# A wider moving side for two small products at the ends of a decode kernel: 448 columns at once, folded back by float32 selecting matmuls

## The chip, the core and the metric

One core of one Trainium2 chip runs the whole program in one launch. The metric is the time of one execution on the device in microseconds (us). A core has TensorE (PE in the profile, its weight loads as PEld), VectorE (DVE), ScalarE (ACT), GpSimd (POOL) and SyncE (SP), which run side by side and wait for one another through semaphores, and 16 DMA engines that bring data from HBM to the on-chip memory SBUF. Matmul results go to PSUM banks.

## What is computed

One decode step for two sequences (B = 2), all in bfloat16 outside the accumulations. A layer norm of x feeds two branches: attention over the last 2,048 positions of a K and a V cache with 16 query heads on 8 key heads of width 256, and a small feed-forward net (FFN). The FFN's output gates that of the attention:

```python
xn = _layernorm(x)                                   # x: 2 x 1 x 448
q  = (xn @ wq)                                       # 16 heads of 256
s  = softmax(q k^T * 256**-0.5) v   @ wo             # last 2048 of 8192 keys; wo: 4096 x 448
g  = silu(relu(xn @ w1) @ w2)                        # w1: 448 x 1792, w2: 1792 x 448
out = x + s * g
```

The caches' part that is read is 8 blocks of 4 MB, and the weights are wq 3.5 MB, w1 and w2 1.5 MB each, and wo 3.5 MB: 44 MB in all, of which every byte is used once.

## The kernel before

The program is a list of operations for each engine, written out by hand: `pr.op` and `pr.dma` append to an engine's list with the operations they depend on, and each engine works through its own list in order. Nothing is planned or reordered by a program.

**The stream of loads.** All large loads go through SP's queue in this order: wq, w1, w2, K block 0, K block 1, V0, K2, V1, K3, V2, V3, and wo in four parts of rows (`WO_PARTS`, a row being 448 numbers on each of 128 partitions). There are two K buffers and two V buffers; V0's buffer holds w1 and w2 first, V1's holds wq. So the issue of V0 waits for the FFN (`st["F"]`), K2 for the last transpose of block 0, V2 for the last product of block 0, and so on. wo is written to K2's buffer and waits for the last transpose of block 2.

**Head.** After the layer norm, `do_q` makes the queries, `do_H` the FFN's hidden layer, `do_hT` turns it, `do_F` (the FFN product with w2) multiplies, and `do_gate` makes silu of it. `do_F` has four column tiles: the array's output columns are split in four groups of 32 partitions, and tile i takes the i-th quarter (112) of the 448 columns. A row of w2 is four matmuls of 112 moving columns, and the result lies with quarter i of sequence b on partition 32i + 16b. The gate is then four operations on 128 x 112. They stand in the middle of block 0: `do_gate()` follows the fifth transpose.

**Four blocks of attention.** For block k, `do_T` transposes K in eight pieces on VectorE, `do_S` makes the scores behind each piece (32 matmuls of 512 columns), `chain` does the softmax (row maximum, its spread by two small matmuls, exponential, transpose), and `do_PV` multiplies with V in 32 matmuls of 512 columns on four column tiles. In `chain(k, pv)` the products with V of the block before stand on TensorE between the softmax's steps. `do_osb`, `do_oT` and `do_at` scale a block's output, fold its heads and spread it into `at_exp`; `do_at` is four VectorE operations of 128 x 16.

**Tail.** After the last V block come `do_PV(3)`, `do_osb`, `do_oT`, `do_at`, two matmuls that gather `at_exp`, a copy `at2`, and the product with wo: 32 rows, each of four matmuls of 112 columns on the four column tiles, accumulated in bank `fbk`. A part of wo is waited for at its first row. Then two VectorE operations (times the gate, plus x) and the store.

```python
for j in range(32):
    deps = deps + [landed.get(j)]
    for i in range(4):
        lo = j * D + i * NCOL
        m_o = pr.op(PE, mm(fbk[32 * i:32 * i + 17, 0:NCOL], view(at2, j, [[2, 17]]),
                           wo_sb[:, lo:lo + NCOL], j == 0, j == 31, tile_position=(0, 32 * i)), deps)
```

Matmuls are recorded by the profile under line 249, that of the helper `mm`, so they are told apart by their tiles.

Of the kernel before, what the change touches and what calls it, by code (L numbers as in the profile page):

```python
# [6 lines left out]
F32 = mybir.dt.float32  # L7
ACT = mybir.ActivationFunctionType
ALU = mybir.AluOpType
AX = mybir.AxisListType  # L10

PE, DVE, ACTE, SP, POOL = "pe", "dve", "act", "sp", "pool"
# [62 lines left out]
def bass_recurrent_scan__sliding_block_cached__dense_activation_relu__decode_kernel(  # L75
# [11 lines left out]
    B, Sq, D = A_x.shape  # L87
# [12 lines left out]
    SLOTS = 7  # L100
    HC = HD // 2
    FC = DFF // 2
    WO_PARTS = [17, 9, 4, 2]
    NCOL = D // 4
    QW = 24 + 8 * 128
    BIG = 1e30
# [2 lines left out]
    with es:  # L109
        pr = _Prog(nc, es)  # L110

        def named(name, shape, dt):
            return es.enter_context(nc.sbuf_tensor(name, shape, dt))

        def psum(name, shape, dt):
            return es.enter_context(nc.psum_tensor(name, shape, dt))

        def view(t, off, dims, n=128, p0=0, pstep=1):
            width = t.shape[1]
            return bass.AP(t, p0 * width + off, [[width * pstep, n]] + dims)  # L120
# [9 lines left out]
        qmask = named("qmask", [128, 4], F32)  # L130
        fold = named("fold", [128, 32], BF)
# [10 lines left out]
        h_n = named("h_n", [128, FC], BF)  # L142
        h_sb = named("h_sb", [128, 32], BF)
        x_c = named("x_c", [128, NCOL], BF)
        ea = named("ea", [128, NCOL], F32)
        g_sb = named("g_sb", [128, NCOL], F32)
        tmp = named("tmp", [128, NCOL], F32)
        out_sb = named("out_sb", [128, NCOL], BF)
# [8 lines left out]
        o_sb = [named(f"o_sb{i}", [128, 512], BF) for i in range(2)]  # L157
        at_exp = named("at_exp", [128, 256], BF)
        at2 = named("at2", [128, 64], BF)
# [3 lines left out]
        wq_sb, w12, wo_sb = vbuf[1], vbuf[0], kbuf[0]  # L163
        W2 = SLOTS * FC
        assert SLOTS * HC <= ROW and W2 + 14 * D <= ROW and 32 * D <= ROW

        sbk = [psum(f"sbk{i}", [128, 512], F32) for i in range(2)]
        obk = [psum(f"obk{i}", [128, 512], F32) for i in range(2)]
        fbk = psum("fbk", [128, 512], F32)
        mbk = psum("mbk", [128, 512], F32)  # L170
        nbk = psum("nbk", [128, 512], F32)
# [18 lines left out]
        def load_v(k):  # L190
            d_v[k] = pr.dma(SP, vbuf[k % 2][:, :], kv_src(k, A_v_cache),
                            [(st["F"], st["q_mm"])[k] if k < 2 else st["PV", k - 2]])
# [7 lines left out]
            out=ident[:, :], in_=ident[:, :], compare_op=ALU.not_equal, fill=1.0,  # L200
# [3 lines left out]
            out=ident_f[:, :], in_=ident_f[:, :], compare_op=ALU.not_equal, fill=1.0,  # L204
            base=0, pattern=[[-1, 128]], channel_multiplier=1), [i1])
        p_one = pr.op(POOL, lambda e: e.memset(one_f[:, :], 1.0), [p_idf])
        p_hz = pr.op(POOL, lambda e: e.memset(h_sb[:, :], 0.0))
# [7 lines left out]
            out=sd[0:B, 0:1], in0=st2[0:B, 1:2], scalar1=EPS, scalar2=None, op0=ALU.add), [v_ag])  # L215
        a_sd = pr.op(ACTE, lambda e: e.activation(sd[0:B, 1:2], sd[0:B, 0:1], ACT.Sqrt), [v_ve])
        v_rs = pr.op(DVE, lambda e: e.reciprocal(rstd[0:B, :], sd[0:B, 1:2]), [a_sd])
        for e2 in range(2):
            v_xn = pr.op(DVE, lambda e, e2=e2: e.tensor_scalar(  # L219
                out=view(xg, 128 - 127 * e2, [[256, 4], [128, 2], [2, 64]], n=B),  # L220
                in0=view(x_sb, 3 * e2, [[1, 4], [0, 2], [SLOTS, 64]], n=B),
# [3 lines left out]
            out=par2[:, :], in_=view(ident, 0, [[1, 2], [2, 64]]), axis=AX.X, op=ALU.add), [p_id])  # L225
# [5 lines left out]
            out=view(wcol, 0, [[4, 128], [1, 4]], n=4), in0=view(ident, 0, [[0, 128], [1, 4]], n=4),  # L231
            scalar1=1.0, scalar2=BIG, op0=ALU.subtract, op1=ALU.mult))
        v_qm = pr.op(DVE, lambda e: e.tensor_reduce(
            out=qmask[:, :], in_=view(ident, 0, [[32, 4], [1, 32]]), axis=AX.X, op=ALU.add))
# [3 lines left out]
                return e.tensor_reduce(out=fold[:, :], in_=view(ident, 0, [[1, 32], [32, 4]]), axis=AX.X, op=ALU.add)  # L238
        v_fold = pr.op(DVE, fold_op)

        def fold8_op(e):
            with nc.allow_low_precision("zeros and ones"):
                return e.tensor_reduce(out=fold8[:, :], in_=view(ident, 0, [[1, 8], [8, 16]]), axis=AX.X, op=ALU.add)
# [4 lines left out]
        def mm(out_ap, lhsT, rhs, start, stop=False, **kw):  # L248
            return lambda e: e.matmul(out_ap, lhsT=lhsT, rhs=rhs, start=start, stop=stop,  # L249
                                      skip_group_check=True, **kw)  # L250

        for s in range(SLOTS):
# [3 lines left out]
            out=view(xr, 0, [[4, SLOTS], [2, 2], [1, 2]]), in0=view(mbk, 0, [[2, SLOTS], [0, 2], [1, 2]]),  # L256
            in1=view(par8, 0, [[1, SLOTS], [1, 2], [0, 2]]), op=ALU.mult), [m_xr, v_par8])

        st = {"mbk": v_xr}
# [28 lines left out]
        def do_qbd(k):  # L288
            deps = [st["qall"], p_qz, st.get(("S", k - 2, 7))]
            for a in range(4):  # L290
                for b in range(2):
                    st["qbd", k] = pr.op(POOL, lambda e, a=a, b=b: e.tensor_copy(  # L292
                        view(qbd[k % 2], 24 + 32 * a + 4 * b, [[2, 2], [128, 8], [1, 2]], n=32, p0=32 * a),
                        view(qall, 32 * k + 16 * b, [[128, 2], [2, 8], [1, 2]], n=32, p0=32 * a)), deps)
                    deps = []
# [12 lines left out]
        def do_hT():  # L308
            deps = [st["h_n"]]
            for j in range(7):  # L310
                o = pr.op(PE, mm(fbk[:, 4 * j:4 * j + 4], view(h_n, j, [[7, 128]], n=4), ident[0:4, 0:4], j == 0), deps)
                deps = []
            st["hT"] = pr.op(DVE, lambda e: e.tensor_copy(
                view(h_sb, 0, [[1, 7], [7, 2], [16, 2]]), view(fbk, 0, [[4, 7], [2, 2], [1, 2]])), [o, p_hz])

        def do_F():
            deps = [d_w2, st["hT"]]
            for f in range(14):
                for i in range(4):
                    lo = W2 + f * D + i * NCOL  # L320
                    o = pr.op(PE, mm(fbk[32 * i:32 * i + 17, 0:NCOL], h_sb[:, f:f + 17],
                                     w12[:, lo:lo + NCOL],
                                     f == 0, f == 13, tile_position=(0, 32 * i)), deps)
                    deps = []
            st["F"] = o

        def do_gate():
            a_e = pr.op(ACTE, lambda e: e.activation(ea[:, :], fbk[:, 0:NCOL], ACT.Exp, scale=-1.0), [st["F"]])
            v_d = pr.op(DVE, lambda e: e.tensor_scalar(
                out=ea[:, :], in0=ea[:, :], scalar1=1.0, scalar2=None, op0=ALU.add), [a_e])  # L330
            v_rc = pr.op(DVE, lambda e: e.reciprocal(tmp[:, :], ea[:, :]), [v_d])  # L331
            st["g"] = pr.op(DVE, lambda e: e.tensor_tensor(
                out=g_sb[:, :], in0=fbk[:, 0:NCOL], in1=tmp[:, :], op=ALU.mult), [v_rc])

        def words(t):
            return t[:, :].bitcast(F32).tensor
# [83 lines left out]
        def do_oT(k):  # L420
            deps = [st["osb", k], v_fold, st["nbk"]]
            for dhi in range(2):
                for t2 in range(2):
                    lo = 256 * t2 + 128 * dhi
                    o = pr.op(PE, mm(nbk[:, 8 * dhi:8 * dhi + 8], o_sb[k % 2][:, lo:lo + 128],
                                     fold[:, 8 * t2:8 * t2 + 8], dhi == 0 and t2 == 0, dhi == 1 and t2 == 1), deps)
                    deps = []
            st["oT", k] = o

        def do_at(k):  # L430
            for b in range(2):
                for h in range(2):
                    st["at", k] = st["nbk"] = pr.op(DVE, lambda e, b=b, h=h: e.tensor_tensor(  # L433
                        out=view(at_exp, 128 * b + 64 * h + 16 * k, [[4, 2], [8, 2], [1, 4]]),
                        in0=view(nbk, 4 * b + 2 * h, [[8, 2], [1, 2], [0, 4]]),
                        in1=view(qmask, 0, [[0, 2], [0, 2], [1, 4]]), op=ALU.mult), [st["oT", k], v_qm])

        def chain(k, pv=None):
            ch_max(k)
# [21 lines left out]
        do_hT()  # L461
        do_F()
        load_v(0)
        do_qbd(0)
        do_qbd(1)
        for e in range(8):
            do_T(0, e)
            do_S(0, e)
            if e == 4:
                do_gate()  # L470
        load_k(2)
        load_v(1)
        for e in range(8):
# [30 lines left out]
        for q in range(8):  # L504
            do_PV(3, q)
        do_osb(3)
        do_oT(3)
        do_at(3)

        d_wo = []  # L510
        j0 = 0
        for n in WO_PARTS:
            d_wo.append((j0, pr.dma(SP, wo_sb[:, j0 * D:(j0 + n) * D], wo_src[:, j0 * D:(j0 + n) * D], [st["T", 2, 7]])))
            j0 += n

        deps = [st["at", NQ - 1], v_fold]
        for b in range(2):
            m_at = pr.op(PE, mm(mbk[:, 256 + 32 * b:288 + 32 * b], at_exp[:, 128 * b:128 * b + 128],
                                fold[:, :], b == 0, b == 1), deps + [st["mbk"]])
            deps = []  # L520
        v_at2 = pr.op(DVE, lambda e: e.tensor_copy(at2[:, :], mbk[:, 256:320]), [m_at])  # L521
        deps = [v_at2, st["g"]]
        landed = dict(d_wo)
        for j in range(32):
            deps = deps + [landed.get(j)]
            for i in range(4):
                lo = j * D + i * NCOL
                m_o = pr.op(PE, mm(fbk[32 * i:32 * i + 17, 0:NCOL], view(at2, j, [[2, 17]]),
                                   wo_sb[:, lo:lo + NCOL],
                                   j == 0, j == 31, tile_position=(0, 32 * i)), deps)  # L530
                deps = []
        v_t = pr.op(DVE, lambda e: e.tensor_tensor(  # L532
            out=tmp[:, :], in0=fbk[:, 0:NCOL], in1=g_sb[:, :], op=ALU.mult), [m_o, st["g"]])
        v_o = pr.op(DVE, lambda e: e.tensor_tensor(  # L534
            out=out_sb[:, :], in0=tmp[:, :], in1=x_c[:, :], op=ALU.add), [v_t, d_xc])
# [33 lines left out]
```

## Time and profile before

| | |
|---|---|
| time, median of 3 runs | 110.56 us (110.33 to 110.9) |
| the profiled execution | 110.73 us |
| its span, first to last instruction | 109.3 us |
| busy in the span | PE 63.9, PEld 26.0, DVE 57.6, ACT 12.4, POOL 9.0 us |
| DMA | 44.19 MB, 404 GB/s over the span |

The span is what the trace covers; 1.43 us of the execution lie around it. A busy time is the union of an engine's instructions, and busy time that runs beside a longer chain costs nothing. In rows of the timeline a bracket tells how long the engine was idle before the row and what released it; "x32" counts instructions that follow one another.

### The profile page before, as it was taken

Reading aid. Unit: us, or ns where it says so; the run is one execution under the profiler, and the core shown is the slowest. Engines: PE = TensorE matmul, PEld = TensorE weight load, DVE = VectorE, ACT = ScalarE, POOL = GpSimd, SP = SyncE. Lnnn points to the kernel's source line nnn. Section 1 sums busy time; section 2 is a strip of 40 time slices with the busy share of each in tenths; the row PEclk is TensorE's granted clock in tenths of the full one; section 3 lists DMA queues with packets and bytes.
Section 4 is the critical chain, followed back from the end, with each engine's and each line's share of the span. In section 5 each row is a group of like instructions: output and inputs, shape, how many; then the busy total and the mean of one; then the engine's idle time right before and its main releaser. Section 6 shows DMA issues by size and latency. Waiting matters only on the chain.

```text
span 109.3 us, 1328 instructions
## 1 busy us (share of the span) xinstructions
PE 63.9 (58%) x554; PEld 26.0 (24%) x554; DVE 57.6 (53%) x95; ACT 12.4 (11%) x24; POOL 9.0 (8%) x45
## 2 busy tenths in 40 slices
PE   0010655764089897849481999683089949009491
PEld 0000113133033222323130334241034214003190
DVE  2165047320399999987435999242399943100202
ACT  2970000000000000200050000032000004100200
POOL 6500000720000004000500000000000000000000
PEclk9999999999556999999996559999959999955559
DMA  6898999999999999999999999999999999999940
GB/s 169 346 483 355 431 404 510 408 432 504 390 396 444 492 396 396 456 480 396 399 480 438 396 408 492 432 396 408 504 420 396 420 498 408 396 405 414 407 171 1
DMA packets 2321, 44.19 MB, mean 404 GB/s; under 512 B 266, under 2 KB 396, under 8 KB 908
## 3 DMA queue, kind: packets, MB, share of 16 engines
q1 hardware_dynamic: 2288, 44.11, 94.6%
q8 instruction: 4, 0.07, 0.2%
q10 hardware_dynamic: 28, 0.01, 0.0%
q14 instruction: 1, 0.01, 0.0%
HBM read 44.11 MB, written 0.00 MB: 403 GB/s over the span
## 4 chain that ended last, share of the span: by engine, by line
DMA 70%; DVE 12%; PE 12%; SPq 3%; issue 1%
DMA kbuf<-in_A_k_cache_dram 42%; DMA kbuf<-in_A_wo_dram 28%; DVE kt L343 10%; PE sbk L249 9%; SPq L36 3%; PE obk L249 2%; DVE tmp L331 1%; DVE rm L361 1%; PE mbk L249 0%; PE nbk L249 0%; PE fbk L249 0%; DVE mx L371 0%; DVE tmp L532 0%; PE mbk L366 0%; DVE out_sb L534 0%
## 5 line engine op out<-in xcount | busy, mean ns | idle before, releaser
L249 PE MATMUL sbk<-kt,qbd 128*128 128x512 bf16 x128 | 36.2, 432 | 15.0 <-DVE kt L343 14.5
L343 DVE STREAM_TRANSPOSE kt<-kbuf 128x1024 f32<-128x1024 f32 x32 | 36.9, 1210 | 8.9 <-DMA kbuf<-in_A_k_cache_dram 8.7
L249 PEld LDWEIGHTS sbk<-kt,qbd 128*128 128x128 bf16 x128 | 12.3, 107 | 37.2 <-DVE kt L343 22.5
L249 PE MATMUL obk<-vbuf,pt 128*16 128x512 bf16 x128 | 9.3, 442 | 4.6 <-DMA vbuf<-in_A_v_cache_dram 4.6
L292 POOL COPY qbd<-qall 32x32 bf16<-32x32 bf16 x32 | 5.7, 204 | 44.1 <-PE sbk L249 28.3
L383 ACT ACTIVATE bias<-mbk 128x1 f32<-128x1 f32 x4 | 0.7, 171 | 58.6 <-PE mbk L249 58.6
L433 DVE TENSOR_TENSOR at_exp<-nbk,qmask 128x16 bf16<-128x16 f32 x16 | 1.7, 166 | 10.5 <-PE nbk L249 10.5
L249 PE MATMUL obk<-vbuf,xr 128*4 128x512 bf16 x28 | 3.2, 626 | 3.8 <-DMA vbuf<-in_A_wq_dram 3.8
L392 DVE STREAM_TRANSPOSE pt<-e_sb 128x512 bf16<-128x512 bf16 x4 | 2.8, 711 | 4.7 <-ACT e_sb L387 4.7
L271 DVE TENSOR_SCALAR kt<-obk 128x1024 bf16<-128x1024 f32 x2 | 2.4, 1218 | 5.6 <-PE obk L249 5.6
L249 PEld LDWEIGHTS obk<-vbuf,pt 128*16 128x16 bf16 x128 | 3.1, 98 | 8.5 <-DMA vbuf<-in_A_v_cache_dram 4.7
L249 PE MATMUL mbk<-ident,xg 2*128 2x2 bf16 x7 | 0.3, 164 | 7.9 <-DVE xg L219 7.9
L361 DVE TENSOR_REDUCE rm<-sbk 128x1 f32<-128x512 f32 x4 | 2.7, 682 | 4.0 <-PE sbk L249 4.0
L249 PE MATMUL fbk<-vbuf,xr 128*4 128x448 bf16 x14 | 4.3, 461 | 0.7 <-DVE h_n L304 0.7
L416 ACT ACTIVATE o_sb<-obk,rs 128x512 bf16<-128x512 f32 x4 | 2.7, 687 | 11.1 <-PE obk L249 11.1
L249 PE MATMUL fbk<-kbuf,at 128*17 128x112 bf16 x128 | 3.1, 282 | 0.4 <-DVE at L521 0.3
L249 PEld LDWEIGHTS fbk<-kbuf,at 128*17 128x17 bf16 x128 | 2.7, 128 | 0.7 <-DVE at L521 0.4
L304 DVE TENSOR_SCALAR h_n<-fbk 4x448 bf16<-4x448 f32 x2 | 1.2, 612 | 3.0 <-PE fbk L249 3.0
L387 ACT ACTIVATE e_sb<-sbk,bias 128x512 bf16<-128x512 f32 x4 | 2.7, 687 | 0.1
L249 PE MATMUL mbk<-one_f,mrow 1*128 1x1 f32 x8 | 1.5, 256 | 1.9 <-DVE mrow L374 1.9
L366 PE MATMUL mbk<-ident_f,rm 128*1 128x128 f32 x4 | 1.1, 270 | 2.4 <-DVE rm L361 2.4
L249 PE MATMUL nbk<-fold,o_sb 128*128 128x8 bf16 x16 | 1.0, 170 | 2.2 <-ACT o_sb L416 2.2
(63 smaller groups left out, 34.4 us busy)
## 6 DMA issues: line engine op xcount, KB each, us to landing
kbuf<-in_A_k_cache_dram SPq DMA_DIRECT2D x4, 4096.0 KB, 27.0
vbuf<-in_A_v_cache_dram SPq DMA_DIRECT2D x4, 4096.0 KB, 26.4
vbuf<-in_A_wq_dram SPq DMA_DIRECT2D x1, 3584.0 KB, 11.2
vbuf<-in_B_w_dram SPq DMA_DIRECT2D x2, 1568.0 KB, 16.2
kbuf<-in_A_wo_dram SPq DMA_DIRECT2D x1, 1904.0 KB, 28.2
kbuf<-in_A_wo_dram SPq DMA_DIRECT2D x1, 1008.0 KB, 30.0
kbuf<-in_A_wo_dram SPq DMA_DIRECT2D x1, 448.0 KB, 30.6
kbuf<-in_A_wo_dram SPq DMA_DIRECT2D x1, 224.0 KB, 30.7
```

The lines of the kernel that those rows point to most:

```text
L36: o = _Op(eng, lambda e: e.dma_start(dst, src), [d for d in deps if d is not None], True)
L249: return lambda e: e.matmul(out_ap, lhsT=lhsT, rhs=rhs, start=start, stop=stop, skip_group_check=True, **kw)
L271: v = pr.op(DVE, lambda e, par=par: e.tensor_scalar(out=view(kt, 128 * par, [[256, 8], [32, 4], [1, 32]]), in0=view(obk[0], par, [[64, 8], ...
L292: st["qbd", k] = pr.op(POOL, lambda e, a=a, b=b: e.tensor_copy(view(qbd[k % 2], 24 + 32 * a + 4 * b, [[2, 2], [128, 8], [1, 2]], n=32, p0= ...
L304: st["h_n"] = pr.op(DVE, lambda e: e.tensor_scalar(out=h_n[0:4, u * (FC // 2):(u + 1) * (FC // 2)], in0=fbk[0:4, 0:FC // 2], scalar1=0.0, ...
L343: st["T", k, e] = pr.op(DVE, lambda e: e.transpose(view(dst, lo, [[128, NT // 2], [1, 32]]), view(src, lo, [[128, NT // 2], [1, 32]])), deps)
L361: st["rm", k] = pr.op(DVE, lambda e: e.tensor_reduce(out=rm[k % 2][:, :], in_=sbk[k % 2][:, :], axis=AX.X, op=ALU.max), [st["S", k, 7], st ...
L366: st["rmT", k] = pr.op(PE, lambda e: e.matmul(mbk[0:1, 0:128], lhsT=rm[k % 2][:, :], rhs=ident_f[:, :], start=True, stop=True, is_transpos ...
L387: st["exp", k] = pr.op(ACTE, lambda e: e.activation(e_sb[k % 2][:, :], sbk[k % 2][:, :], ACT.Exp, bias=bias[k % 2][:, 0:1], accum_out=ssum ...
L392: st["pt", k] = pr.op(DVE, lambda e: e.transpose(pt[k % 2][:, :], e_sb[k % 2][:, :]), [st["exp", k], st.get(("PV", k - 2))])
L416: st["osb", k] = pr.op(ACTE, lambda e: e.activation(o_sb[k % 2][:, :], obk[k % 2][:, :], ACT.Copy, scale=rs[:, k:k + 1]), [st["PV", k], st ...
L433: st["at", k] = st["nbk"] = pr.op(DVE, lambda e, b=b, h=h: e.tensor_tensor(out=view(at_exp, 128 * b + 64 * h + 16 * k, [[4, 2], [8, 2], [1 ...
```

## The change

- `do_F` takes all 448 columns as one matmul for each of the 14 rows of w2, with no column tiles. The result lies on two partitions. The gate's four operations run on 2 x 448, and four float32 matmuls with a selecting matrix `sel` (0 and 1) bring it to the layout of before, where ScalarE copies it. `do_gate()` now follows `do_F()` directly, ahead of block 0.
- The product with wo takes its first 16 rows (`WO_WIDE`) with 448 columns: row j goes to column tile j mod 4, so that four rows run on the four tiles, into the score bank `sbk[0]`. ScalarE copies that bank to `wsum`; ahead of row 28 four float32 matmuls with `sel` add the four partial sums to `fbk`. Rows 16 to 31 stay as they were.
- `do_at` is one VectorE operation of 128 x 64; `do_oT` writes its columns in another order for it.
- wo comes in parts of 16, 10, 4, 2 rows in place of 17, 9, 4, 2.

```diff
-    WO_PARTS = [17, 9, 4, 2]
+    WO_PARTS = [16, 10, 4, 2]
+    WO_WIDE = 16
...
+        v_sz = pr.op(DVE, lambda e: e.memset(sel[:, :], 0.0))
+        v_sel = pr.op(DVE, lambda e: e.tensor_copy(view(sel, 0, [[16, 2]]), fold[:, 0:2]), [v_fold, v_sz])
...
         def do_F():
             deps = [d_w2, st["hT"]]
             for f in range(14):
-                for i in range(4):
-                    lo = W2 + f * D + i * NCOL
-                    o = pr.op(PE, mm(fbk[32 * i:32 * i + 17, 0:NCOL], h_sb[:, f:f + 17],
-                                     w12[:, lo:lo + NCOL],
-                                     f == 0, f == 13, tile_position=(0, 32 * i)), deps)
-                    deps = []
+                o = pr.op(PE, mm(fbk[0:2, 0:D], h_sb[:, 2 * f:2 * f + 2],
+                                 w12[:, W2 + f * D:W2 + (f + 1) * D], f == 0, f == 13), deps)
+                deps = []
...
         def do_gate():
-            a_e = pr.op(ACTE, lambda e: e.activation(ea[:, :], fbk[:, 0:NCOL], ACT.Exp, scale=-1.0), [st["F"]])
+            a_e = pr.op(ACTE, lambda e: e.activation(ea[:, :], fbk[0:2, 0:D], ACT.Exp, scale=-1.0), [st["F"]])
...
+            for i in range(4):
+                o = pr.op(PE, mm(fbk[32 * i:32 * i + 17, 0:NCOL], sel[0:2, :],
+                                 g2[:, i * NCOL:(i + 1) * NCOL], True, True, tile_position=(0, 32 * i)), deps)
+                deps = []
+            st["g"] = pr.op(ACTE, lambda e: e.activation(g_sb[:, :], fbk[:, 0:NCOL], ACT.Copy), [o])
...
         def do_at(k):
-            for b in range(2):
-                for h in range(2):
-                    st["at", k] = st["nbk"] = pr.op(DVE, lambda e, b=b, h=h: e.tensor_tensor(
-                        out=view(at_exp, 128 * b + 64 * h + 16 * k, [[4, 2], [8, 2], [1, 4]]),
-                        in0=view(nbk, 4 * b + 2 * h, [[8, 2], [1, 2], [0, 4]]),
-                        in1=view(qmask, 0, [[0, 2], [0, 2], [1, 4]]), op=ALU.mult), [st["oT", k], v_qm])
+            st["at", k] = st["nbk"] = pr.op(DVE, lambda e: e.tensor_tensor(
+                out=view(at_exp, 16 * k, [[64, 4], [4, 4], [1, 4]]),
+                in0=view(nbk, 0, [[4, 4], [1, 4], [0, 4]]),
+                in1=view(qmask, 0, [[0, 4], [0, 4], [1, 4]]), op=ALU.mult), [st["oT", k], v_qm])
...
         load_v(0)
+        do_gate()
...
             do_S(0, e)
-            if e == 4:
-                do_gate()
...
-        for j in range(32):
-            deps = deps + [landed.get(j)]
+        wbk = sbk[0]
+        deps.append(st["exp", 2])
+        for r in range(WO_WIDE // 4):
+            deps = deps + [landed.get(4 * r)]
+            for i in range(4):
+                j = 4 * r + i
+                m_w = pr.op(PE, mm(wbk[32 * i:32 * i + 2, 0:D], view(at2, j, [[32, 2]]),
+                                   wo_sb[:, j * D:(j + 1) * D],
+                                   r == 0, 4 * (r + 1) == WO_WIDE, tile_position=(0, 32 * i)), deps)
+                deps = []
+        a_ws = pr.op(ACTE, lambda e: e.activation(wsum[:, :], wbk[:, 0:D], ACT.Copy), [m_w])
+        for j in range(WO_WIDE, 32):
+            deps = [landed.get(j)]
+            if j == 28:
+                for i in range(4):
+                    pr.op(PE, mm(fbk[32 * i:32 * i + 17, 0:NCOL], sel[:, :], wsum[:, i * NCOL:(i + 1) * NCOL],
+                                 False, tile_position=(0, 32 * i)), [a_ws])
             for i in range(4):
```

More of the change, by code (lines that the diff above doesn't have):

```diff
@@ L144, in bass_recurrent_scan__sliding_block_cached__dense_activation_relu__decode_kernel @@
         x_c = named("x_c", [128, NCOL], BF)
-        ea = named("ea", [128, NCOL], F32)
+        ea = named("ea", [2, D], F32)
+        g2 = named("g2", [2, D], F32)
+        sel = named("sel", [128, 17], F32)
+        wsum = named("wsum", [128, D], F32)
         g_sb = named("g_sb", [128, NCOL], F32)
@@ L313, in do_hT @@
             st["hT"] = pr.op(DVE, lambda e: e.tensor_copy(
-                view(h_sb, 0, [[1, 7], [7, 2], [16, 2]]), view(fbk, 0, [[4, 7], [2, 2], [1, 2]])), [o, p_hz])
+                view(h_sb, 0, [[2, 7], [14, 2], [1, 2]]), view(fbk, 0, [[4, 7], [2, 2], [1, 2]])), [o, p_hz])
         def do_F():
@@ L318, in do_F @@
             for f in range(14):
-                for i in range(4):
-                    lo = W2 + f * D + i * NCOL
-                    o = pr.op(PE, mm(fbk[32 * i:32 * i + 17, 0:NCOL], h_sb[:, f:f + 17],
-                                     w12[:, lo:lo + NCOL],
-                                     f == 0, f == 13, tile_position=(0, 32 * i)), deps)
-                    deps = []
+                o = pr.op(PE, mm(fbk[0:2, 0:D], h_sb[:, 2 * f:2 * f + 2],
+                                 w12[:, W2 + f * D:W2 + (f + 1) * D], f == 0, f == 13), deps)
+                deps = []
             st["F"] = o
         def do_gate():
-            a_e = pr.op(ACTE, lambda e: e.activation(ea[:, :], fbk[:, 0:NCOL], ACT.Exp, scale=-1.0), [st["F"]])
+            a_e = pr.op(ACTE, lambda e: e.activation(ea[:, :], fbk[0:2, 0:D], ACT.Exp, scale=-1.0), [st["F"]])
             v_d = pr.op(DVE, lambda e: e.tensor_scalar(
                 out=ea[:, :], in0=ea[:, :], scalar1=1.0, scalar2=None, op0=ALU.add), [a_e])
-            v_rc = pr.op(DVE, lambda e: e.reciprocal(tmp[:, :], ea[:, :]), [v_d])
-            st["g"] = pr.op(DVE, lambda e: e.tensor_tensor(
-                out=g_sb[:, :], in0=fbk[:, 0:NCOL], in1=tmp[:, :], op=ALU.mult), [v_rc])
+            v_rc = pr.op(DVE, lambda e: e.reciprocal(g2[:, :], ea[:, :]), [v_d])
+            v_g2 = pr.op(DVE, lambda e: e.tensor_tensor(
+                out=g2[:, :], in0=fbk[0:2, 0:D], in1=g2[:, :], op=ALU.mult), [v_rc])
+            deps = [v_g2, v_sel]
+            for i in range(4):
[3 more added lines that the diff above has]
+            st["g"] = pr.op(ACTE, lambda e: e.activation(g_sb[:, :], fbk[:, 0:NCOL], ACT.Copy), [o])
         def words(t):
@@ L424, in do_oT @@
                     lo = 256 * t2 + 128 * dhi
-                    o = pr.op(PE, mm(nbk[:, 8 * dhi:8 * dhi + 8], o_sb[k % 2][:, lo:lo + 128],
+                    o = pr.op(PE, mm(view(nbk, dhi, [[2, 8]]), o_sb[k % 2][:, lo:lo + 128],
                                      fold[:, 8 * t2:8 * t2 + 8], dhi == 0 and t2 == 0, dhi == 1 and t2 == 1), deps)
@@ L529, in bass_recurrent_scan__sliding_block_cached__dense_activation_relu__decode_kernel @@
                                    wo_sb[:, lo:lo + NCOL],
-                                   j == 0, j == 31, tile_position=(0, 32 * i)), deps)
+                                   j == WO_WIDE, j == 31, tile_position=(0, 32 * i)), deps)
                 deps = []
```

## The prediction

> **What bounds the kernel now.** I read the page first: how full the DMA is, and what the last chain consists of.
>
> ```profile
> PE 63.9 (58%) x554; PEld 26.0 (24%) x554; DVE 57.6 (53%) x95; ACT 12.4 (11%) x24; POOL 9.0 (8%) x45
> ...
> DMA  6898999999999999999999999999999999999940
> ...
> q1 hardware_dynamic: 2288, 44.11, 94.6%
> q8 instruction: 4, 0.07, 0.2%
> ...
> DMA 70%; DVE 12%; PE 12%; SPq 3%; issue 1%
> ```
>
> SP's queue (q1) holds the 16 DMA engines 94.6% of the span, and no slice between the second and the 38th falls under 8 tenths. The kernel is its stream of loads, plus what stands ahead of it and behind it. An edit counts where it makes the stream run dry or lengthens what follows its end. So the chain of waits comes next, at its end:
>
> ```profile
> 75.50 0.43 SPq L36
> 75.93 0.04 issue
> 75.98 30.68 DMA kbuf<-in_A_wo_dram
> 106.65 0.04 issue
> 106.70 0.30 PE fbk L249 x8
> ```
>
> The last part of wo (2 rows) lands at 106.65, and eight matmuls, the two VectorE operations and the store close the kernel. How close is TensorE to being the later of the two? The timeline of the tail:
>
> ```profile
> 98.14 3.59 PE L249 MATMUL obk<-vbuf,pt 128*16 128x512 bf16 x32 [4.59 <-DMA vbuf<-in_A_v_cache_dram]
> ...
> 101.78 0.69 ACT L416 ACTIVATE o_sb<-obk,rs 128x512 bf16<-128x512 f32 x1 [8.54 <-PE obk L249]
> ...
> 102.83 0.42 DVE L433 TENSOR_TENSOR at_exp<-nbk,qmask 128x16 bf16<-128x16 f32 x4 [8.83 <-PE nbk L249]
> ...
> 103.58 0.22 DVE L521 CAST at<-mbk 128x64 bf16<-128x64 f32 x1 [0.33 <-PE mbk L249]
> ...
> 103.86 3.12 PE L249 MATMUL fbk<-kbuf,at 128*17 128x112 bf16 x128 [0.32 <-DVE at L521]
> 106.70 0.11 PEld L249 LDWEIGHTS fbk<-kbuf,at 128*17 128x17 bf16 x8 [0.23 <-DMA kbuf<-in_A_wo_dram]
> ```
>
> The chain behind V3 (products, scaling, fold, spread, copy) lets the wo product start at 103.86, and 30 of its 32 rows are through when TensorE waits 0.23 us for the last part. That 0.23 us is the slack on which everything hangs: the stream's end and TensorE's work end practically together. Two more things about the tail, from the windows (us; busy of each engine; then PE clock, DMA share, GB/s):
>
> ```profile
> 104.85:105.35 0.50, 0.50 (x36) 0.50 (x28) 0.00 (x0) 0.00 (x0) 0.00 (x0) 0.50 0.43 140
> 105.35:105.85 0.50, 0.50 (x32) 0.50 (x28) 0.00 (x0) 0.00 (x0) 0.00 (x0) 0.50 0.22 86
> 105.85:106.28 0.43, 0.43 (x32) 0.43 (x24) 0.00 (x0) 0.00 (x0) 0.00 (x0) 0.51 0.08 29
> 106.28:106.50 0.22, 0.22 (x24) 0.18 (x16) 0.00 (x0) 0.00 (x0) 0.00 (x0) 1.00 0.00 0
> ```
>
> TensorE's granted clock is 0.50 until 106.28 and 1.00 after. And the stream does not stop at once: most DMA engines are done by 105.3, and a few (86, then 29 GB/s; the mean rate of 404 is 25 for each of 16) end up to 1.3 us later.
>
> **The wide rows cost what the narrow ones did.** The question is what one matmul of 448 columns on one of four tiles costs beside four of 112.
>
> ```profile
> 98.53 0.14 PEld L249 LDWEIGHTS obk<-vbuf,pt 128*16 128x16 bf16 x4 [0.28 <-issue]
> 98.95 0.14 PEld L249 LDWEIGHTS obk<-vbuf,pt 128*16 128x16 bf16 x4 [0.28 <-issue]
> ...
> 71.87 1.90 PE L249 MATMUL obk<-vbuf,pt 128*16 128x512 bf16 x32
> ```
>
> The products with V have exactly the wide form: four tiles, 512 columns. At half clock a group of four starts every 0.42 us, 0.83 ns a column; at full clock eight groups take 1.90 us with the drain of the last, 0.21 us each, 0.42 ns a column. So the four tiles stream side by side. A wide group, four rows, is 448 x 0.83 = 0.37 us at half clock. Four narrow rows are 4 x 112 = 448 columns too, 0.37 us; 30 of them from 103.86 to 106.47 is 0.087 us a row, which is 0.093 for all but the last few. 16 rows are 1.49 us either way: fewer instructions, the same stream of columns, no gain.
>
> **The spread of the block's output.** Four operations took 0.42; one of 64 elements from PSUM is nearest to the copy of 64 beside it, 0.22. Bounds are 0.17 (one of the four with its drain) and 0.42. I take 0.22: wo's product starts 0.20 earlier, at 103.66. In the three other blocks this lies ahead of waits for K and V and brings nothing.
>
> **The fold is new work on TensorE**, behind row 27, thus after part three, and ahead of rows 28 to 31. Part three's landing:
>
> ```profile
> kbuf<-in_A_wo_dram SPq DMA_DIRECT2D x1, 448.0 KB, 30.6
> ```
>
> 75.50 + 30.6 = 106.1. Rows 0 to 15 end at 105.15, rows 16 to 25 at 106.08, rows 26 and 27 at 106.29. ScalarE's copy of 448 columns has from 105.35 (with some 0.2 of drain) to there; by the 512 columns of the scaling (0.69) it is done at 106.05, covered by 0.24. Now the float32 matmuls:
>
> ```profile
> L249 PE MATMUL fbk<-vbuf,h_sb 128*17 128x112 bf16 x56 | 0.9, 213 | 0.5 <-DVE h_sb L313 0.5
> ...
> 70.67 0.27 PE L366 MATMUL mbk<-ident_f,rm 128*1 128x128 f32 x1 [0.78 <-DVE rm L361]
> ...
> 71.56 0.38 PE L249 MATMUL mbk<-one_f,mrow 1*128 1x1 f32 x2 [0.62 <-DVE mrow L374]
> ```
>
> A float32 piece of 128 columns took 0.27 us where a bfloat16 one of 112 took 0.213 at full clock. 16 columns more are 0.007, so the other 0.05, about 120 columns' time, says two cycles a column. And a true float32 matmul is recorded as two pieces (x2 for one matmul). So one fold matmul is 2 pieces x 112 x 2 x 0.42 = 0.19 us at full clock, 0.37 at half. For the four tiles there are three orders: side by side, 0.19 in all; the second piece of a tile waiting for its first while the next tile's first runs beside it, 5 steps of 0.094 = 0.47; or all eight in a row, 0.75. At half clock 0.37, 0.94, 1.50. These are the bounds, since no float32 matmul on tiles is in the trace. I take 0.47: matmuls are issued in order, the two pieces use the same tile, and by the V products' rows different tiles overlap.
>
> The sum: the clock rises at 106.28, the fold runs from 106.29 to 106.76, rows 28 and 29 (0.047 each) to 106.85, and the last two rows start there in place of 106.70: **+0.15 us**. 0.20 us saved ahead and 0.23 us of slack are spent on 0.47 of fold and the wait of rows 26 and 27 for part three. The profiled execution's 110.73 becomes 110.88; it lies 0.17 above the median of the runs shown, so on the median the forecast is **110.7**. The split of wo in 16 and 10 rows moves no wait: row 16 is reached long after.
>
> **The head costs nothing, as long as the stream covers it.**
>
> ```profile
> 21.64 1.49 PE L249 MATMUL fbk<-vbuf,xr 128*4 128x448 bf16 x7 [0.71 <-DVE h_n L304]
> ...
> 24.83 0.87 PE L249 MATMUL fbk<-vbuf,h_sb 128*17 128x112 bf16 x56 [0.47 <-DVE h_sb L313]
> ...
> 29.20 5.75 DVE L343 STREAM_TRANSPOSE kt<-kbuf 128x1024 f32<-128x1024 f32 x5 [4.52 <-DMA kbuf<-in_A_k_cache_dram]
> ...
> 34.88 0.18 DVE L329 TENSOR_SCALAR ea<-ea 128x112 f32<-128x112 f32 x1
> 35.09 0.85 DVE L331 RECIPROCAL tmp<-ea 128x112 f32<-128x112 f32 x1
> 35.98 0.27 DVE L332 TENSOR_TENSOR g_sb<-fbk,tmp 128x112 f32<-128x112 f32 x1
> ...
> 39.68 0.54 SPq L36 DMA_DIRECT2D kbuf<-in_A_k_cache_dram  x1
> ```
>
> Untiled, the FFN's rows stream one after another: seven of this shape took 1.49, so 14 take 2.98 in place of 0.87, and it ends at 27.8. ScalarE's exponential of 448 columns is at most 0.69, to 28.5. On VectorE the three gate operations took 1.30 on 112 columns and grow at most fourfold, 5.2, to 33.7. The transposes of block 0, which began at 29.20 when K0 landed, are queued behind them, at most 4.5 later, and no longer have the 1.3 in their midst: 3.2 late at most. TensorE's four selecting matmuls wait for the same product, with block 0's scores queued behind, which need the first transpose anyway. K2's issue, 39.68, waits for the last one: 42.9 at most, with V1's issue behind it on SP. Is the stream dry by then?
>
> ```profile
> 0.00:39.68 39.68, 18.59 (x157) 6.96 (x157) 19.57 (x32) 5.88 (x8) 6.12 (x29) 0.91 0.97 410
> ```
>
> By 39.68 the stream has moved 410 x 39.68 = 16.3 MB; wq, w1, w2, K0, K1 and V0, all issued, are 19.5 MB. 3.2 MB, 7.8 us, are still queued: 4.6 us to spare, and beyond that each us of lateness would be a us of the end. VectorE then catches up where it waits for K blocks:
>
> ```profile
> 78.39 9.13 DVE L343 STREAM_TRANSPOSE kt<-kbuf 128x1024 f32<-128x1024 f32 x8 [3.11 <-DMA kbuf<-in_A_k_cache_dram]
> ```
>
> Its 3.11 us of idle time before block 3 is about the 3.2 at most. VectorE's two new operations for `sel` are some 0.4 us in the start, before wq has landed.
>
> **Rivals.** *The clock stays at half through the fold* (slower). The place is rows 0 to 31 and the fold. It decides when the clock rises after 106.28, here the very moment the fold is due. Price: fold 0.94 to 107.23, two rows to 107.42, and the last pair 0.09 slower: 0.72 + 0.09 = 0.81 us, 111.4. For it: the clock rose only at the end of 2.4 us of unbroken rows. Against: it did rise. The Trainium skill ("TensorE: Matmul & The Clock Gate", part 1, on the HAM clock gate) says that the windows in which activity is judged run free of the kernel, about 3.4 us each, so that the point of the rise differs from run to run; by that rule some runs pay this price, and the single rise seen here agrees with it without showing it. Chance 0.18.
>
> *The fold's eight pieces run in a row.* At full clock 0.75, so 0.43 late, 111.0; at half clock 1.36 late, 111.9. For it: nothing shows float32 on tiles. Chance 0.14, of which 0.09 at half clock.
>
> *The fold is side by side*: 0.19, everything hidden, 110.6. Chance 0.13.
>
> *Instruction loads fall elsewhere.* The queue q8 moved four packets between the loads; one of them, in the window from 58 to 60 us:
>
> ```profile
> q8 instruction: 1, 0.02, 3.0%
> ```
>
> 3.0% of 16 engines x 2 us is 0.96 us of one engine, and the stream's ragged end (a few engines up to 1.3 us late) is what three such delays would leave. The change takes 42 + 48 narrow matmuls out and adds 16 float32 pieces, 74 fewer of the 554 on the page's first line, each with its weight load, so packets that follow the program's progress come at other times, and on whichever DMA engines. Two on one engine: the last landing 0.96 later, 111.5, chance 0.10. One fewer, or none so late: up to 0.96 earlier, with V3's landing and all behind it, 109.6 to 110.3, and most of that is faster; chance 0.13. Against both: the program gets only an eighth shorter, so about three packets should still lie in the stream. The Trainium skill ("Runtime: NRT & Kernel Launch", on instruction fetch) says that an engine's program is fetched in blocks of 256 instructions as it is worked through; by that figure TensorE's would be 4.3 blocks before and 3.75 after, an estimate, and the trace's four packets agree with the first.
>
> The forecast itself has 0.32. The change does what its text says; I see no rival there.
>
> **How the numbers follow.** A difference of 0.5%, 0.55 us, is about what a measurement of this kernel can tell from none. Within it lie the forecast (0.32), the hidden fold (0.13) and the row of eight at full clock (0.05): 0.50. Slower: half clock 0.18, row of eight at half clock 0.09, two fetches on one engine 0.10: 0.37. Faster: 0.13. The range from 110.0 to 111.6 leaves out most of the last, 0.1, and the 111.9.
>
> **What would show it.** wo's product starting about 0.2 earlier behind the last V; groups of four wide matmuls 0.37 apart at half clock; eight float32 pieces in some 0.47 us, and the granted clock at that moment; TensorE no longer waiting for wo's last part; K2 issued some 2 to 3 us later with the DMA slices still full. The forecast is wrong if the last landing moves by more than 0.5 us, if the fold takes over 0.9, or if a DMA slice near 45 us falls.

## The result, and the profile after

Over nine runs each, the changed kernel takes 111.54 us (111.18 to 112.01) and the kernel before 110.61 us (110.33 to 111.13). The ratio, which is reckoned from all of these runs, is 1.0062, with a 95% interval of 1.004 to 1.0085: by it the change costs 0.7 us, where the two medians lie 0.93 apart. The profiled execution took 112.01 us, span 110.5; it is the slowest of the nine, so its rows are read for durations, and what the change costs is read from the ratio.

The page: the stream still fills the span, and the chain now ends in TensorE and VectorE work.

```profile
DMA packets 2320, 44.17 MB, mean 400 GB/s; under 512 B 266, under 2 KB 396, under 8 KB 780
...
q1 hardware_dynamic: 2288, 44.11, 93.8%
q8 instruction: 3, 0.05, 0.2%
...
DMA 36%; PE 32%; DVE 26%; issue 2%; ACT 1%; SPq 1%
```

The tail in the timeline (start, duration, instructions; in brackets the idle time before and its releaser):

```profile
98.92 3.26 PE L256 MATMUL obk<-vbuf,pt 128*16 128x512 bf16 x32 [4.28 <-DMA vbuf<-in_A_v_cache_dram]
...
103.28 0.23 DVE L441 TENSOR_TENSOR at_exp<-nbk,qmask 128x64 bf16<-128x64 f32 x1 [8.38 <-PE nbk L256]
...
104.09 0.93 PE L256 MATMUL sbk<-kbuf,at 128*2 128x448 bf16 x16 [0.32 <-DVE at L528]
105.07 0.54 ACT L541 ACTIVATE wsum<-sbk 128x448 f32<-128x448 f32 x1 [2.15 <-PE sbk L256]
...
106.00 1.45 PE L256 MATMUL fbk<-kbuf,at 128*17 128x112 bf16 x48 [0.98 <-DMA kbuf<-in_A_wo_dram]
...
107.24 0.59 PE L256 MATMUL fbk<-wsum,sel 128*17 128x112 f32 x8
...
107.61 0.59 PE L256 MATMUL fbk<-kbuf,at 128*17 128x112 bf16 x16
108.25 0.27 DVE L554 TENSOR_TENSOR tmp<-fbk,g_sb 128x112 f32<-128x112 f32 x1 [4.21 <-PE fbk L256]
```

The same operation behind the last row, in the kernel before:

```profile
107.03 0.28 DVE L532 TENSOR_TENSOR tmp<-fbk,g_sb 128x112 f32<-128x112 f32 x1 [3.23 <-PE fbk L249]
```

Two differences stand out. V3's products start at 98.92 where they started at 98.14: the last V block is 0.78 us later before the tail begins. And from there to the first closing operation it takes 9.33 us where it took 8.89. The wide rows ran at full clock here (16 rows in 0.93), then TensorE waited 0.98 us for wo's second part and went on at half clock:

```profile
104.00:105.00 1.00, 0.91 (x16) 0.30 (x16) 0.04 (x1) 0.00 (x0) 0.00 (x0) 1.00 0.92 357
105.00:105.50 0.50, 0.02 (x4) 0.00 (x0) 0.00 (x0) 0.43 (x1) 0.00 (x0) 0.62 0.34 133
105.50:106.00 0.50, 0.00 (x0) 0.00 (x0) 0.00 (x0) 0.12 (x1) 0.00 (x0) 0.50 0.25 100
106.00:106.50 0.50, 0.50 (x24) 0.50 (x28) 0.00 (x0) 0.00 (x0) 0.00 (x0) 0.50 0.20 79
```

(The columns are as in the windows before: TensorE's clock, DMA share and GB/s are the last three.) In the head, the FFN product and the gate are much longer than before, and K2 is issued late:

```profile
26.09 4.73 PE L256 MATMUL fbk<-vbuf,h_sb 128*2 128x448 bf16 x14 [0.37 <-DVE h_sb L320]
...
31.85 2.94 DVE L335 RECIPROCAL g<-ea 2x448 f32<-2x448 f32 x1
...
35.36 10.23 DVE L353 STREAM_TRANSPOSE kt<-kbuf 128x1024 f32<-128x1024 f32 x9
...
44.50 0.54 SPq L36 DMA_DIRECT2D kbuf<-in_A_k_cache_dram  x1
```

So there were three suspects: the late head, the fold at the end, and whatever makes the stream end later.

### The profile page after: what moved, and what is told of

Its sections match the earlier page's. It is cut to its first block, busy times and chain, and to the rows that moved or that the text cites. A ratio compares the mean times of both kernels' runs of the same rounds, so it can differ in the third digit from the quotient of the medians.

```text
span 110.5 us, 1172 instructions
## 1 busy us (share of the span) xinstructions
PE 68.3 (62%) x480; PEld 26.4 (24%) x480; DVE 59.3 (54%) x85; ACT 13.5 (12%) x26; POOL 9.1 (8%) x45
## 4 chain that ended last, share of the span: by engine, by line
DMA 36%; PE 32%; DVE 26%; issue 2%; ACT 1%; SPq 1%
DMA kbuf<-in_A_wo_dram 26%; DVE kt L353 15%; PE fbk L256 12%; PE sbk L256 12%; DMA vbuf<-in_A_wq_dram 10%; PE obk L256 6%; DVE g L335 3%; DVE kt L278 2%; DVE rm L371 2%; PE nbk L256 1%; DVE h_n L311 1%; PE mbk L256 1%; SPq L36 1%; DVE mx L381 1%; ACT o_sb L426 1%
## 5 line engine op out<-in xcount | busy, mean ns | idle before, releaser
L256 PE MATMUL sbk<-kt,qbd 128*128 128x512 bf16 x128 | 35.0, 427 | 6.8 <-DVE kt L353 6.6
L441 DVE TENSOR_TENSOR at_exp<-nbk,qmask 128x64 bf16<-128x64 f32 x4 | 0.9, 224 | 10.1 <-PE nbk L256 10.1
L256 PE MATMUL fbk<-vbuf,xr 128*4 128x448 bf16 x14 | 5.5, 573 | 0.7 <-DVE h_n L311 0.7
L256 PE MATMUL fbk<-vbuf,h_sb 128*2 128x448 bf16 x14 | 4.7, 519 | 0.4 <-DVE h_sb L320 0.4
L256 PE MATMUL fbk<-g,sel 2*17 2x112 f32 x8 | 0.6, 378 | 4.7 <-DVE g L336 4.7
L332 ACT ACTIVATE ea<-fbk 2x448 f32<-2x448 f32 x1 | 0.5, 533 | 23.2 <-PE fbk L256 23.2
L335 DVE RECIPROCAL g<-ea 2x448 f32<-2x448 f32 x1 | 2.9, 2941 | 0.0
```

Of the source, the lines that this page charges most:

```text
L335: v_rc = pr.op(DVE, lambda e: e.reciprocal(g2[:, :], ea[:, :]), [v_d])
```

## The experiments

Each was compared with the kernel before on its own chip, in five rounds.

**First set: the parts of the change alone, and the fold moved.**

*The head alone* (`do_F`, `do_gate`, its place, `sel`):

```diff
+        load_v(0)
+        do_gate()
...
-            if e == 4:
-                do_gate()
```

> Only the head of the change: the FFN product with 448 moving columns, the gate on two partitions, its four selecting matmuls, and the gate ahead of block 0. The tail is that of before. If the loss lies in the tail (the fold behind wo's late rows), this equals before within 0.2 us, with K2 issued some 4 to 5 us later (44.5 in the changed kernel, 39.7 before) and the last V landing where it did. If the late head thins the load stream, it carries most of the 0.7 us, and the last V block lands some 0.5 us or more later.

Measured: 111.13 us, ratio 1.0041 (1.0029 to 1.0053). Slower without any change in the tail. Neither description fits the profile: K2 is issued at 41.28, only 1.6 us later than before, and V3's products start at 98.37, 0.23 us later.

*The tail alone* (`WO_WIDE`, the fold, the parts of wo, `sel` and `wsum`), with the head and spread of before:

> Only the tail of the change: wo in 16, 10, 4, 2 rows, the first 16 with 448 columns, the fold ahead of row 28; head and spread of before. If the fold is the loss, 0.4 to 0.8 us slower than before, with the VectorE operation behind the last row some 0.4 us or more later after the last V landing's start of products than before (8.89 us there). If the loss is the head's, within 0.2 us of before.

Measured: 111.24 us, ratio 1.0058 (1.0045 to 1.007). From V3's products to the operation behind the last row it takes 9.26 us, 0.37 more than before; but V3's products themselves start 0.22 later, at 98.36, and no fold can do that.

*The spread and the parts of wo alone*:

```diff
-    WO_PARTS = [17, 9, 4, 2]
+    WO_PARTS = [16, 10, 4, 2]
...
+            st["at", k] = st["nbk"] = pr.op(DVE, lambda e: e.tensor_tensor(
+                out=view(at_exp, 16 * k, [[64, 4], [4, 4], [1, 4]]),
```

> Only the spread in one operation and wo's parts of 16, 10, 4, 2, all 32 rows narrow. By both theories within 0.2 us of before: wo's product starts 0.2 us earlier and waits 0.2 us longer for its last part.

Measured: 110.56 us, ratio 0.9994 (0.9985 to 1.0002). The time is as forecast. So is the start of wo's product, 5.49 us after V3's products where it took 5.72 in before:

```profile
98.03 3.59 PE L249 MATMUL obk<-vbuf,pt 128*16 128x512 bf16 x32 [3.52 <-DMA vbuf<-in_A_v_cache_dram]
...
102.71 0.23 DVE L431 TENSOR_TENSOR at_exp<-nbk,qmask 128x64 bf16<-128x64 f32 x1 [7.95 <-PE nbk L249]
...
103.52 0.97 PE L249 MATMUL fbk<-kbuf,at 128*17 128x112 bf16 x64 [0.32 <-DVE at L519]
...
106.53 0.28 PE L249 MATMUL fbk<-kbuf,at 128*17 128x112 bf16 x8 [0.16 <-DMA kbuf<-in_A_wo_dram]
106.86 0.28 DVE L530 TENSOR_TENSOR tmp<-fbk,g_sb 128x112 f32<-128x112 f32 x1 [3.39 <-PE fbk L249]
```

TensorE's granted clock was 1.00 through these rows, and 0.50 in the profile of before, so how long it waits for wo's parts can't be compared between the two.

*The fold ahead of row 24*:

```diff
-            if j == 28:
+            if j == 24:
```

> The changed kernel with the fold ahead of row 24 in place of row 28, so that it stands before the wait for wo's third part. If the fold behind that wait is the loss, 0.3 to 0.5 us faster than the changed kernel, near 111.1 or less. If the stream's later end is, no difference from the changed kernel, 111.5.

Measured: 111.35 us, ratio 1.0067 (1.0055 to 1.0079). Taking the fold out of the last wait brought nothing.

Both theories fell. The head alone costs 0.41% and the tail alone 0.58%, but together 0.62%: they do not add up, as if each brought the whole of one loss. What the three slow kernels share, and the fast one lacks, is not work but new tensors in SBUF ahead of the K and V buffers: `sel` and `wsum` in all three, and in two of them also `g2` and a longer `ea`. Tensors are laid one behind the other, so the K buffers start at 39168 bytes (153 x 256) in before and with the spread alone, at 44192 in the changed kernel, with the head alone and with the fold ahead of row 24, at 41056 with the tail alone; the last two are 32 past a multiple of 64. The trace's DMA records show it: of the 1,024 packets of 32 KB that carry K and V, 991 took 1213 ns to the nanosecond in before and 1,019 with the spread alone. In the three slow ones 206 to 219 did, and 202 in the changed kernel; but for three or four in each, the rest took 1214 to 1226.

**Second set: only the buffers' start moved.** An unused tensor of 32 bytes stands ahead of the K buffers and moves them, the V buffers and `kt`, the only tensors behind it, in the kernel before (which gets the misplaced start) and in three others (which get a multiple of 64).

```diff
+        named("pad", [128, 16], BF)
         kbuf = [named(f"kbuf{i}", [128, ROW], BF) for i in range(2)]
```

> The kernel before with an unused tensor of 32 bytes a partition ahead of the K buffers, and nothing else: the buffers of the load stream start at 39200 in place of 39168, 32 past a multiple of 64 as in the changed kernel. If the start of the buffers is the loss, some 0.4 us slower than before (111.0), and the K and V packets, 1213 ns nearly all in before, spread to 1222. If the loss is the later instruction loads or the late head, no change (110.6).

Measured: 111.47 us, ratio 1.0055 (1.0036 to 1.0075), with not one instruction changed. Of the packets 16 took 1213 ns; the commonest times were 1216 and 1224. The page's DMA line and the tail:

```profile
DMA packets 2321, 44.19 MB, mean 402 GB/s; under 512 B 266, under 2 KB 396, under 8 KB 908
```

```profile
98.55 3.59 PE L250 MATMUL obk<-vbuf,pt 128*16 128x512 bf16 x32 [4.46 <-DMA vbuf<-in_A_v_cache_dram]
...
107.26 0.12 PEld L250 LDWEIGHTS fbk<-kbuf,at 128*17 128x17 bf16 x8 [0.27 <-DMA kbuf<-in_A_wo_dram]
107.68 0.28 DVE L533 TENSOR_TENSOR tmp<-fbk,g_sb 128x112 f32<-128x112 f32 x1 [3.47 <-PE fbk L250]
```

V3's products start 0.41 us later than in before and wo's last part is awaited until 107.26, not 106.70. The engines' work on the moved buffers did not grow: a transpose of K took 1211 ns on average, 1210 in before. It is the loads that took longer.

> The changed kernel with an unused tensor of 32 bytes a partition ahead of the K buffers, which start at a multiple of 64 again. If the start of the buffers costs some 0.4 us and the fold the rest, 110.8 to 111.0. If the fold or the late head is all of the loss, 111.3 as the changed kernel.

Measured: 111.45 us, ratio 1.0056 (1.0034 to 1.0079): not better.

> The changed kernel with the fold ahead of row 24 and the buffers at a multiple of 64. If the buffers' start and the fold behind the last waits are all of the loss, within 0.2 us of before (110.6). If the stream's end moves for another reason, 111.2 or more.

Measured: 111.46 us, ratio 1.0047 (1.0025 to 1.0069).

> Only the head of the change, as in the first run of it, with the buffers at a multiple of 64. If the buffers' start was its loss, 110.6, the time of before, though K2 is still issued 4 to 5 us later. If the late head thins the stream, 111.1 as in that run.

Measured: 111.34 us, ratio 1.0037 (1.0017 to 1.0057). A multiple of 64 changed nothing: these buffers start at 44224, 192 past a multiple of 256, and only 111 to 166 packets took 1213 ns. Either the start must be a multiple of more than 64 (the third set tries 256; no run tries 128), or the theory covers only part of it.

**Third set: a multiple of 256, or not.** The kernel before with 64 bytes ahead of the buffers (39232), and the three others with 96 bytes (44288 = 173 x 256).

```diff
+        named("pad", [128, 32], BF)     # before
+        named("pad", [128, 48], BF)     # the three others
         kbuf = [named(f"kbuf{i}", [128, ROW], BF) for i in range(2)]
```

> The kernel before with an unused tensor of 64 bytes a partition ahead of the K buffers, which start at 39232, 64 past a multiple of 256 (39168 in before). If a multiple of 64 is enough, 110.6 to 110.9, the time of before, and K and V packets of 1213 ns; if it takes 256, as slow as with 32 bytes, some 0.5% above before, with packets of 1215 and more.

Measured: 111.39 us, ratio 1.0054 (1.003 to 1.0077). 64 is not enough. This is also the control for the three below, which ran on the same chip.

> The changed kernel with an unused tensor of 96 bytes a partition ahead of the K buffers, which start at 44288, a multiple of 256 as in before. If the buffers' start is most of the loss, the packets are 1213 ns again and the time is 0.1 to 0.3% above before, what is left being the fold behind the last waits. If the work itself is the loss, 0.6% above before as it was.

Measured: 110.85 us, ratio 1.0014 (0.9986 to 1.0041).

```profile
DMA packets 2320, 44.17 MB, mean 405 GB/s; under 512 B 266, under 2 KB 396, under 8 KB 780
```

```profile
97.80 3.59 PE L257 MATMUL obk<-vbuf,pt 128*16 128x512 bf16 x32 [4.21 <-DMA vbuf<-in_A_v_cache_dram]
...
103.33 1.67 PE L257 MATMUL sbk<-kbuf,at 128*2 128x448 bf16 x16 [0.32 <-DVE at L529]
...
106.10 0.45 PE L257 MATMUL fbk<-wsum,sel 128*17 128x112 f32 x8
...
106.38 0.37 PE L257 MATMUL fbk<-kbuf,at 128*17 128x112 bf16 x16
106.80 0.27 DVE L555 TENSOR_TENSOR tmp<-fbk,g_sb 128x112 f32<-128x112 f32 x1 [3.53 <-PE fbk L257]
```

> The same with the fold ahead of row 24. If the buffers' start and the fold behind the last waits are all of the loss, within 0.15% of before. If not, 0.4% or more above it.

Measured: 111.04 us, ratio 1.0018 (0.9991 to 1.0044). Its interval does not tell the fold at row 24 from that at row 28.

> Only the head of the change, with the buffers at a multiple of 256. If the head's loss was the buffers' start, the time of before within 0.15%, though K2 is issued 4 to 5 us later. If the late head thins the stream, 0.4% above before as in the two runs of it.

Measured: 110.72 us, ratio 0.9999 (0.9977 to 1.0021). The head costs nothing, with K2 issued at 41.47. That is 1.8 us later than before, not the 4 to 5 of the expectation, which were read from the changed kernel's profile:

```profile
24.99 2.81 PE L256 MATMUL fbk<-vbuf,h_sb 128*2 128x448 bf16 x14 [0.37 <-DVE h_sb L320]
...
28.82 2.94 DVE L335 RECIPROCAL g<-ea 2x448 f32<-2x448 f32 x1
...
41.47 0.54 SPq L36 DMA_DIRECT2D kbuf<-in_A_k_cache_dram  x1
...
97.95 3.59 PE L256 MATMUL obk<-vbuf,pt 128*16 128x512 bf16 x32 [3.07 <-DMA vbuf<-in_A_v_cache_dram]
```

All kernels in one table. "Stream" is worked out from the DMA records: the time from the landing of w2 to that of wo's last part in the profiled execution, each taken as the mean of the first eight of its 16 landings, one for each DMA engine. This leaves out the engines that come last.

| kernel | K buffers start at | past a multiple of 256 | packets of 1213 ns | stream, us | ratio to before |
|---|---|---|---|---|---|
| before | 39168 | 0 | 991 | 86.16 | 1 |
| spread and parts alone | 39168 | 0 | 1019 | 86.14 | 0.9994 |
| changed, 256 | 44288 | 0 | 1019 | 86.15 | 1.0014 |
| fold at 24, 256 | 44288 | 0 | 1019 | 86.08 | 1.0018 |
| head alone, 256 | 44288 | 0 | 1018 | 86.14 | 0.9999 |
| changed | 44192 | 160 | 202 | 86.40 | 1.0062 |
| head alone | 44192 | 160 | 207 | 86.54 | 1.0041 |
| tail alone | 41056 | 96 | 219 | 86.52 | 1.0058 |
| fold at 24 | 44192 | 160 | 206 | 86.48 | 1.0067 |
| before + 32 bytes | 39200 | 32 | 16 | 86.57 | 1.0055 |
| changed + 32 bytes | 44224 | 192 | 166 | 86.53 | 1.0056 |
| fold at 24 + 32 bytes | 44224 | 192 | 138 | 86.52 | 1.0047 |
| head alone + 32 bytes | 44224 | 192 | 111 | 86.50 | 1.0037 |
| before + 64 bytes | 39232 | 64 | 116 | 86.55 | 1.0054 |

The two groups do not overlap in any of the last three columns. The stream is 86.08 to 86.16 us at a multiple of 256 and 86.40 to 86.57 off it, 0.4 us apart on average. The packets account for most of it: in before with 32 bytes a K or V packet took 4.4 ns longer on average (the few above 1400 ns left out), which over the 64 of each DMA engine is 0.28 us, and wo's packets add 0.10, of a stream that is 0.41 longer. With 64 bytes the two are 0.28 together, of 0.39. The Trainium skill ("DMA: Bandwidth & Descriptors", on how a descriptor splits into AXI transactions) says that a transaction has to start at a multiple of 256 bytes, so that a run that doesn't is cut into one more. The page speaks of what is read, and here it is the destination in SBUF that was moved; that the cut is the mechanism is argued from there, not shown.

Two things in the records limit the theory. No off start that was tried is a multiple of 128, so the runs agree with 256 without singling it out. One load speaks for 128: wo's second part in before starts 15232 bytes into its buffer, 128 past a multiple of 256, and 123 of its 128 packets took 305 ns; with 32 and 64 bytes ahead of the buffers 7 and 27 did, and they averaged 311 to 312. And a start off the multiple is not enough by itself: wq, w1 and w2 go into the same V buffers, yet w1's 128 packets took 469 ns each in all fourteen profiles. Why only K, V and wo are slowed stays open.

## Why the prediction was right or wrong, point by point

The measured 111.54 lies in the range, but that is luck: the sum that led to 110.7 missed the largest term. **The step that failed** is the first: an edit counts "where it makes the stream run dry or lengthens what follows its end". There is a third way. The stream itself can slow down, by where its buffers lie, and every load was priced as in before. Adding three tensors (`sel`, `g2`, `wsum`) and enlarging `ea` moved the buffers off a multiple of 256. By the runs this is 0.55% in the kernel before, and 0.3 to 0.4% between the same kernel on and off the multiple (1.0056 to 1.0014, 1.0047 to 1.0018, 1.0037 to 0.9999, each pair from two chips). The rivals held no such case; the range covered it because it was wide for others.

**What is left of the change is near what the sum said.** With the buffers at a multiple of 256 it costs 0.14%, 0.15 us, where the sum gave +0.15. Its interval (-0.14% to +0.41%) reaches to nothing, and one of the terms came out otherwise (the fold, below), so the agreement in the second digit is chance.

- *The wide rows*: no gain, as forecast. 16 rows took 1.67 us at half clock with their drain (1.49 in the sum) and 0.93 at full.
- *The spread*: 0.23 measured, 0.22 taken, and in the changed kernel at 256 wo's product starts 5.53 us after V3's products, 0.19 earlier than before. Alone it gains nothing, as forecast.
- *The fold was mis-sized*: 0.47 taken, 0.37 at half clock measured (107.24 to 107.61, where row 28 starts) and 0.19 at full, in the changed kernel with 32 bytes:

```profile
106.52 0.36 PE L257 MATMUL fbk<-wsum,sel 128*17 128x112 f32 x8
...
106.71 0.55 PE L257 MATMUL fbk<-kbuf,at 128*17 128x112 bf16 x16
```

  That is the lower bound in both clocks: the four tiles run side by side, and two pieces of one tile do not hold up the next tile. Two cycles a column and two pieces for a matmul held, and the order that came is the rival that was given 0.13; it wasn't all hidden, because the clock was not at full throughout. At a multiple of 256 the clock rose within the fold (0.70 on average from 106.10 to 106.38), at the moment that the sum had taken from before, and the fold took 0.28.
- *The head is covered*: the head alone at 256 shows it for a K2 issued 1.8 us late. But the bound "42.9 at most" for K2's issue was broken: 44.50 in the changed kernel's profile. The FFN's rows were priced by a row at full clock, 2.98. They took 2.81 in six of the nine profiles with this head, and 4.73 to 5.14 in the other three. In the changed kernel's, eleven rows fall in the first 3.9 us, nearly the 0.37 apart of the half clock, though the profile gives the clock there as 1.00. The slack of 4.6 us behind 42.9 took up this lateness too: K2 landed 9.72 us after V0 (mean of the first eight landings), as V0 had after K1 (9.71), and the DMA slices stay full.
- *The clock at half through the fold* came in the changed kernel's profile, after a wait for wo's second part, and cost less than its 0.81, since the fold is 0.37 and not 0.94 there. In that rival the trigger was wrong too: the clock had risen before wo's product began and fell in the wait.
- *Instruction loads elsewhere*: the packets went from four to three and came at other times, as the smaller count of matmuls said. With the head alone at 256 they come later too, and the time is that of before; with 32 bytes ahead of before's buffers they come as in before, and the loss is there. So this is not where the loss of the medians was, though the rival's 111.5 is close to the measured time.
- *A sign of being wrong came*: the last landing, 107.61 in the changed kernel's profile and 106.65 in that of before, moved by 0.96 us, more than the 0.5 allowed. Of this, 0.40 is in the mean of the first eight landings (105.36 and 104.96), the rest in the engines that come last.

Open: the stream explains some 0.4 us, and before with 32 or 64 bytes loses 0.6; the intervals (0.3 to 0.77%) allow either. V3's 0.78 us in the changed kernel's profile are 0.32 in the mean of its first eight landings, near what the buffers explain, and the rest in the engines that come last; what held those up was not followed up, and that execution is the slowest of nine. The tail alone was not run at a multiple of 256, so the price of the fold without the buffers' loss is known only together with the head.

None of the kernels beats the one before: the spread alone, and at 256 the head alone, the changed kernel and the one with the fold at row 24, stand within their intervals of it.

## What to carry to other kernels

In a kernel bound by its stream of loads, a new small tensor can cost more than the work it serves: look at where the large buffers start, and keep them at a multiple of 256 bytes, with a filler if need be (a smaller multiple, 128, may do, but was not tried). If two halves of a change each cost as much as the whole, look for something that they share and that isn't work. And where the stream's end and the last matmuls meet, shortening the matmuls' side alone gained nothing here.

## What the runs showed of the hardware

- In SBUF buffers that start off a multiple of 256 bytes most 32 KB packets of K and V took 1214 to 1226 ns where nearly all took 1213 at the multiple, at offsets of 32, 64, 96, 160 and 192 alike; the stream from w2 to wo is 0.2 to 0.5 us longer, and the kernels are 0.3 to 0.6% slower than at the multiple. The packets of w1 into the same buffers were not slowed (469 ns everywhere). An offset of 128 was not tried for K and V.
- A float32 matmul runs as two pieces of two cycles a column, on four column tiles side by side: eight pieces of 112 columns took 0.19 us at full clock and 0.37 at half.
- VectorE's reciprocal goes by columns: 2.94 us for 448 of them on two partitions, where 112 on 128 partitions took 0.85.
